# A channel-attention kernel on one core: 398 of 1152 rows kept on chip instead of 392, and the second pass in another order

## The chip, the cores and the metric

The kernel runs on one core of one Trainium2 chip. The metric is the device time of one execution in microseconds (us); a profiled execution also has a trace, whose own span is a little shorter than that execution's time.

## The reference

```python
x: [1, 384, 384, 384] bfloat16      # H x W positions, 384 channels
w1d: [1] bfloat16                   # a one-tap filter over the channels
g = einsum("bhwc->bc", x) / (H * W) # mean of each channel
s = sigmoid(g * w1d[0])
out = x * s[:, None, None, :]
```

Every value of x is needed for s, and every value of x is needed again, times s, for the output.

## The kernel before, in words

x is laid out as 1152 **rows**: one row is 384 channels in each of the 128 partitions, 768 bytes per partition and 98,304 bytes in all. A tile of "128x18432" elements is 48 rows of 384.

**Pass one** loads all 1152 rows. TensorE multiplies each row by a matrix of ones and accumulates the channel sums in one PSUM bank (`sum_rows`, line 292). Rows that stay on chip for pass two are loaded last into their own places, the others pass through ("streamed"). ScalarE then computes s (`s_bf`, line 513).

**Pass two** writes all 1152 rows times s. Rows that were kept are multiplied on VectorE (`scale`, line 527; three pieces on GpSimd) and stored. Streamed rows have to be loaded a second time, into places that stores have set free, multiplied and stored.

**Kept rows** are of two kinds. Raw rows lie as they came. Folded rows lie in groups: three rows w0, w1, w2 take up the bits of a fourth row u, since some exponent bits of the data are nearly always the same. So four rows occupy three, and u's place may be used for something else. `fold` does this in pass one for a **piece** of four u rows (16 rows): VectorE tests (`test`, a TENSOR_SCALAR of line 327, written to Y), makes two fields (line 327, in T) and joins them (line 333), twice; after each test ScalarE sums the tested values into `seen` (line 364), and the next test has to wait for that, since it writes the same place Y. `unfold` takes a piece apart again in pass two. If a test ever failed, GpSimd does the folded rows again at the end (`verdict`, `again`); with this data it does not.

**Places.** `arena` holds the groups, the raw rows and work places T and Y (eight rows each); `annex` is a block of 20 more rows in what is otherwise scratch memory for software DMA. Groups stand in two columns; the bits that one group (BANKED) saves are kept in PSUM, and a last group EXTRA shares the place A.. with it. U, V and W are the u rows of groups 7, 8 and EXTRA, refilled with raw rows after the fold.

**Order.** All DMAs are issued by SP in the order in which the program records them, on one queue. A load waits for the readers of its place, a store for its scaling, and whatever stands behind a waiting DMA waits too. In pass one the order is written out by hand (`BETWEEN`, `group`). In pass two a planner (the `while True` loop) decides it at build time, from modelled costs (`ROW`, `LAT`, ...) and `RULES`: how large a run of free rows must be to be loaded (at most `CAP`), how long the backlog must be, and in how large parts a load is scaled (`PARTS_OF`). The groups are unfolded in the list `order`.

Of the kernel before, what the change touches and what calls it, by code (L numbers as in the profile page):

```python
# [145 lines left out]
def kernel(  # L146
# [11 lines left out]
    nc = tc.nc  # L158
    P = nc.NUM_PARTITIONS
# [11 lines left out]

    PIECE = 4
    PAIR = 2 * PIECE
    PAIRS = 4
# [3 lines left out]
    A = V + PAIR  # L178
    N_A = 39
    T = A + N_A  # L180
# [7 lines left out]
    for i in range(PAIRS):  # L188
# [21 lines left out]
    pieces = [  # L210
        (g, lo, min(m, q - lo))
        for g, (_, q) in enumerate(GROUPS) for m in [q if g == BANKED else PIECE] for lo in range(0, q, m)
    ]

    ones = pool.tile([P, P], bf16, name="ones")
    w_bf = pool.tile([1, 1], bf16, name="w_bf")
    w_sc = pool.tile([P, 1], f32, name="w_sc")
    worst = pool.tile([P, 1], f32, name="worst")
    odd = pool.tile([P, 1], bf16, name="odd")
    arena = pool.tile([P, ROWS, C], bf16, name="arena")  # L220
    annex = nc.alloc_sbuf_tensor_at("annex", [P, N_X, C], bf16, offset=RING).ap()
    s_bf = pool.tile([P, C], bf16, name="s_bf")
    zeros = pool.tile([P, P], bf16, name="zeros")
    seen = pool.tile([P, 2 * len(pieces)], f32, name="seen")
    odd_i = pool.tile([P, 1], mybir.dt.int32, name="odd_i")
# [4 lines left out]
    CUT = C - C // 3  # L230
    tail = bank0[:, nc.PSUM_BANK_SIZE_BYTES // 4 - (C - CUT) // 2 :].bitcast(bf16)
# [5 lines left out]
    assert BANK * len(banks) - PS * C >= CUT  # L237
    spare = banks[-1][:, BANK - CUT :]

    def view(t, r0, n):  # L240
# [5 lines left out]
    def rows(lo, n):  # L246
        return [("a", r) for r in range(lo, lo + n)]
# [88 lines left out]
    def flat(a, p):  # L336
        return arena[:, a : a + p, :].bitcast(u16)
# [4 lines left out]

    def fold(k, T=T, Y=Y):

        g, lo, p = pieces[k]
        first, q = GROUPS[g]
        a, ua = first + 3 * lo, first + 3 * q + lo
        wc = [rows(a + j * p, p) for j in range(3)]
        u, uc = flat(ua, p), rows(ua, p)
        t, tc2 = flat(T, 2 * p), rows(T, 2 * p)  # L350

        def field(i, op, by, mask):
            bits(flat(T + i * p, p), u, op, by, AND, mask, uc, rows(T + i * p, p))

        def test(i, parts):

            at = Y
            for first, n in parts:
                bits(flat(at, n), flat(first, n), AND, 0x7800, XOR, 0x3800, rows(first, n), rows(at, n))
                at += n  # L360
            y = flat(Y, 2 * p)
            fl.add(
                "ACT",
                lambda: nc.scalar.activation(  # L364
                    out=y, in_=y, func=ACTF.Copy, accum_out=seen[:, 2 * k + i : 2 * k + i + 1]
                ),
                reads=rows(Y, 2 * p), writes=rows(Y, 2 * p) + [("seen", 2 * k + i)],
            )

        test(0, [(a, 2 * p)])  # L370
        field(0, SHL, 7, 0x7800)
        field(1, SHL, 11, 0x7800)
        w01 = flat(a, 2 * p)
        join(w01, w01, t, XOR, wc[0] + wc[1] + tc2, wc[0] + wc[1])
        test(1, [(a + 2 * p, p), (ua, p)])
        field(0, SHL, 3, 0x3800)
        field(1, SHR, 1, 0x4000)
        w2 = flat(a + 2 * p, p)
        for i in range(2):
            join(w2, w2, flat(T + i * p, p), XOR, wc[2] + rows(T + i * p, p), wc[2])  # L380


    N_DVE, N_SP = (62, 14), 32

# [67 lines left out]
    PARTS = ((0, CUT, spare, "spare"), (CUT, C, tail, "bank0"))  # L452
    S1, S2, S3 = [(A, 19)], [(A + 19, 19)], [(X, N_X)]

# [8 lines left out]
    def group(g, where):  # L463

        if isinstance(where, list):
            take(g)
            for k in of_group(g):
                fold(k)
            stream_all(where)
        else:  # L470
            k1, k2 = of_group(g)
            take(g, 0, 12)
            take(g, 24, 32)
            fold(k1)
            stream_all(where[0])
            take(g, 12, 24)
            fold(k2)
            stream_all(where[1])

    BETWEEN = [  # L480
        (2, LOW_COLUMN + HIGH), (4, [(A, 38)]),
        (5, [(G0 - 24, 24), (A - 24, 24), *S3]),
        (6, (S1, S2)), (7, ([(A - 24, 24)], S1)),
        (8, (S3, S2)), (EXTRA, []),
    ]
# [18 lines left out]

    for a, n in [(X, N_X), (U, 8), (V, 8), (W + 4, 8), (W + 12, 8), (W + 20, 7), (W, 4), (T, 4), (T + 4, 4), (Y, 4), (Y + 4, 2), (Y + 6, 2)]:
        step = take_raw(a, n)
        if a == Y - 4:
            fl.hold("DVE", 2 * N_DVE[1], step)
# [4 lines left out]
        lambda: nc.scalar.activation(out=s_bf[:], in_=acc, func=ACTF.Sigmoid, scale=w_sc[:, 0:1]),  # L513
        reads=["bank0", "w_sc"], writes=["s_bf"],
    )
# [77 lines left out]
    def verdict():  # L593

        fl.add(
            "DVE",
            lambda: nc.vector.tensor_reduce(out=worst[:], in_=seen[:], op=Op.max, axis=mybir.AxisListType.X),
            reads=[("seen", k) for k in range(2 * len(pieces))], writes=["worst"],
        )
        fl.add(  # L600
            "DVE",
            lambda: nc.vector.tensor_single_scalar(out=odd[:], in_=worst[:], scalar=0.0, op=Op.is_gt),  # L602
            reads=["worst"], writes=["odd"],
        )
        fl.add(
            "PE",
            lambda: nc.tensor.matmul(votes, lhsT=ones[:], rhs=odd[:], start=True, stop=True),  # L607
            reads=["ones", "odd"], writes=["bank0"],
        )
# [8 lines left out]
    def again():  # L618
# [28 lines left out]
    RULES = [  # L647
        (80, 48, 8.0, 24, 9.0, 4.0, 3.5),
        (190, 40, 2.5, 14, 3.0, 5.0, 6.0),
        (430, 64, 6.0, 33, 9.0, 4.0, 2.0),  # L650
        (N_STREAM, 24, 6.0, 33, 16.0, 7.0, 6.0),
    ]
    PARTS_OF = (16, 48)
    BANKS_AT = 2
    N_SPLIT, N_WHOLE = 2, 4
    now = dve_at = 0.0
# [49 lines left out]

    for a, n, end in ((Y, 2, True), (Y + 2, 2, True), (Y + 4, 4, True), (V, 4, True), (V + 4, 4, True), (T, 8, True), (X, 10, True), (X + 10, 10, True), (U, 8, True)):
        landed.append((a, raw(a), n, end))
    landed.append((W, raw(W), 8, True))
    landed.append((W + 8, raw(W + 8), 6, True))  # L710


    alongside = deque()
    t = 1.0
    for a, n in ((A + 26, 4), (A + 30, 4), (A + 34, 5)):
# [70 lines left out]
    while True:  # L786
        MANY, SHORT, FEW, AMPLE, LOW, LAST = next(r[1:] for r in RULES if todo <= r[0])

# [52 lines left out]
        if got and todo < N_STREAM:  # L841
            n, a = max(got)
            left = N_STREAM - todo
            left -= run_of(left - 1)[0]
            n = min(n, CAP, left)
            ahead = backlog()
            behind = storing and sum(m for m, _ in got) < MANY and ahead >= SHORT
            if not behind and (todo or not (landed or alongside or waiting)) and (n >= min(BIG, left) and (n == left or left > CAP) or (ahead < LOW and n >= 8) or ahead < LAST):
                storing = False

                lo = N_STREAM - todo - n
                load(lo, a, n)
                for i in range(a, a + n):
                    idle[i] = False
                parts = [(a + e, lo + e, f - e, f == n) for e, f in split(n, PARTS_OF[not line and not turns])]
                todo += n
                moves.append([now + LAT, n * ROW + PER_LOAD, lambda parts=parts: landed.extend(parts)])
# [45 lines left out]
```

## Time and profile before

| | before |
|---|---|
| median of 3 runs | 713.63 us (713.4 to 714.04) |
| profiled execution: its time, its span | 714.23 us, 712.4 us |
| DMA: bytes, mean rate over the span | 301.34 MB, 423 GB/s |
| read from HBM, written to it | 187.96 MB, 113.25 MB |
| busy: DMA queue of SP / VectorE / TensorE / ScalarE | 99% / 67% / 30% / 17% |

The bytes read are 1152 rows for pass one and 760 for pass two; the bytes written are 1152 rows. The page gives engine shares over the whole span; the two passes have to be told apart by windows of time. "DMA share" is the mean busy share of the 16 DMA engines; it can stand a little above 1.

### The profile page before, as it was taken

Reading aid. Unit: us, or ns where it says so; the run is one execution under the profiler, and the core shown is the slowest. Engines: PE = TensorE matmul, PEld = TensorE weight load, DVE = VectorE, ACT = ScalarE, POOL = GpSimd, SP = SyncE. Lnnn points to the kernel's source line nnn. Section 1 sums busy time; section 2 is a strip of 40 time slices with the busy share of each in tenths; the row PEclk is TensorE's granted clock in tenths of the full one; section 3 lists DMA queues with packets and bytes.
Section 4 is the critical chain, followed back from the end, with each engine's and each line's share of the span. In section 5 each row is a group of like instructions: output and inputs, shape, how many; then the busy total and the mean of one; then the engine's idle time right before and its main releaser. Section 6 shows DMA issues by size and latency. Waiting matters only on the chain.

```text
span 712.4 us, 2053 instructions
## 1 busy us (share of the span) xinstructions
PE 214.5 (30%) x1186; PEld 0.3 (0%) x3; DVE 476.3 (67%) x371; ACT 121.6 (17%) x97; POOL 10.2 (1%) x7
## 2 busy tenths in 40 slices
PE   4686968888887880000000000000000000000000
PEld 0000000000000000000000000000000000000000
DVE  3608250347968947959899989979258914897460
ACT  3706140235746730000000200000000000000000
POOL 0000000000000005000000000000000000000000
PEclk9898989999999995555555555555555555555555
DMA  9999999999999998999999999999999999999997
GB/s 370 443 418 440 429 433 433 433 429 432 426 427 428 434 389 346 393 427 423 430 431 434 428 439 439 430 419 435 445 433 428 437 435 433 430 436 433 425 436 311
DMA packets 17727, 301.34 MB, mean 423 GB/s; under 512 B 1971, under 2 KB 2483, under 8 KB 5811
## 3 DMA queue, kind: packets, MB, share of 16 engines
q1 hardware_dynamic: 17712, 301.21, 99.0%
q8 instruction: 4, 0.07, 0.0%
q14 instruction: 9, 0.07, 0.0%
q10 hardware_dynamic: 2, 0.00, 0.0%
HBM read 187.96 MB, written 113.25 MB: 423 GB/s over the span
## 4 chain that ended last, share of the span: by engine, by line
DMA 71%; DVE 16%; PE 7%; ACT 2%; SPq 0%; issue 0%; DVEq 0%
DMA arena<-in_x_dram 47%; DMA out_dram<-arena 19%; DVE arena L527 10%; PE bank L292 7%; DMA annex<-in_x_dram 3%; DVE arena L327 2%; ACT arena L364 2%; DVE annex L527 2%; DVE arena L333 1%; DMA out_dram<-annex 1%; SPq L286 0%; ACT s_bf L513 0%; SPq L541 0%; SPq L898 0%; DVEq L124 0%
## 5 line engine op out<-in xcount | busy, mean ns | idle before, releaser
L527 DVE TENSOR_TENSOR arena<-arena,s_bf 128x6144 bf16<-128x6144 bf16 (+9 forms) x69 | 212.1, 3114 | 84.4 <-DMA arena<-in_x_dram 73.1
L292 PE MATMUL bank<-arena,ones 128*128 128x384 bf16 x1091 | 197.3, 343 | 39.2 <-DMA arena<-in_x_dram 38.4
L327 DVE TENSOR_SCALAR arena<-arena 128x1536 uint16<-128x1536 uint16 (+4 forms) x198 | 136.9, 745 | 105.5 <-DMA arena<-in_x_dram 97.7
L364 ACT ACTIVATE arena<-arena 128x3072 uint16<-128x3072 uint16 (+1 forms) x38 | 107.6, 2831 | 105.6 <-DVE arena L327 105.5
L607 PE MATMUL bank<-odd,ones 128*128 128x1 bf16 x1 | 0.2, 187 | 385.9 <-DVE odd L602 385.9
L333 DVE TENSOR_TENSOR arena<-arena 128x1536 uint16<-128x1536 uint16 (+3 forms) x83 | 106.6, 1284 | 9.2 <-PE bank L292 6.2
L445 ACT COPY arena<-bank 128x512 uint32<-128x512 uint32 (+3 forms) x9 | 4.5, 497 | 127.1 <-DMA out_dram<-arena 126.9
L527 DVE TENSOR_TENSOR annex<-annex,s_bf 128x3840 bf16<-128x3840 bf16 x6 | 12.7, 2153 | 10.5 <-DMA annex<-in_x_dram 10.5
L527 POOL TENSOR_TENSOR arena<-arena,s_bf 128x1536 bf16<-128x1536 bf16 (+1 forms) x3 | 10.0, 3356 | 268.6 <-ACT bank L517 268.6
L292 PE MATMUL bank<-annex,ones 128*128 128x384 bf16 x60 | 11.9, 361 | 4.5 <-DMA annex<-in_x_dram 4.5
L445 ACT COPY bank<-arena 128x512 uint32<-128x512 uint32 (+3 forms) x9 | 4.1, 491 | 35.8 <-PE bank L292 35.8
L527 DVE TENSOR_TENSOR arena<-arena,bank 128x1536 bf16<-128x1536 bf16 (+2 forms) x7 | 8.2, 1232 | 0.0
L364 ACT ACTIVATION_READ_ACCUMULATOR arena<-arena 128x1 f32 x38 | 7.1, 186 | 0.0
L292 PE MATMUL bank<-zeros,ones 128*128 128x384 bf16 x32 | 5.5, 326 | 0.0
L527 DVE TENSOR_TENSOR annex<-annex,bank 128x3840 bf16<-128x3840 bf16 x2 | 4.2, 2145 | 0.0
L306 PE MATMUL bank<-arena,ones 128*128 128x384 bf16 x1 | 0.5, 479 | 7.8 <-DMA arena<-in_x_dram 7.8
L513 ACT ACTIVATE s_bf<-bank,w_sc 128x384 bf16<-128x384 f32 x1 | 0.6, 581 | 9.7 <-PE bank L292 9.7
L871 ACT ACT_TABLE_LOAD x1 | 1.3, 1283 | 0.7 <-PEq L887 0.7
L396 DVE TENSOR_SCALAR w_sc<-bank 128x1 f32<-128x1 f32 x1 | 0.2, 159 | 1.1 <-PE bank L391 1.1
L386 DVE MEMSET ones<- 128x128 bf16 x1 | 0.2, 165 | 1.0 <-SPq L118 1.0
L391 PE MATMUL bank<-w_bf,ones 1*128 1x1 bf16 x1 | 0.2, 182 | 2.1 <-DMA w_bf<-in_w1d_dram 2.1
L607 PEld LDWEIGHTS bank<-odd,ones 128*128 128x128 bf16 x1 | 0.1, 105 | 643.6 <-DVE odd L602 643.6
(11 smaller groups left out, 1.5 us busy)
## 6 DMA issues: line engine op xcount, KB each, us to landing
arena<-in_x_dram SPq DMA_DIRECT2D x17, 4608.0 KB, 30.2
out_dram<-arena SPq DMA_DIRECT2D x7, 4608.0 KB, 30.0
out_dram<-arena SPq DMA_DIRECT2D x6, 3072.0 KB, 33.0
arena<-in_x_dram SPq DMA_DIRECT2D x5, 3072.0 KB, 15.2
arena<-in_x_dram SPq DMA_DIRECT2D x6, 2304.0 KB, 20.9
annex<-in_x_dram SPq DMA_DIRECT2D x6, 1920.0 KB, 11.0
arena<-in_x_dram SPq DMA_DIRECT2D x2, 4512.0 KB, 25.9
out_dram<-arena SPq DMA_DIRECT2D x2, 4512.0 KB, 18.6
```

The lines of the kernel that those rows point to most:

```text
L292: return pe.add_instruction(mybir.InstMatmult(name=nc.get_next_instruction_name(), ins=[pe.lower_ap(rhs), pe.lower_ap(ones[:])], outs=[pe. ...
L306: return nc.tensor.matmul(acc, lhsT=ones[:], rhs=mem(i, 1)[:, 0, :], start=first, stop=last)
L327: lambda: nc.vector.tensor_scalar(out=dst, in0=src, scalar1=s0, scalar2=s1, op0=op0, op1=op1),
L333: "DVE", lambda: nc.vector.tensor_tensor(out=dst, in0=a, in1=b, op=op), reads=reads, writes=writes
L364: lambda: nc.scalar.activation(out=y, in_=y, func=ACTF.Copy, accum_out=seen[:, 2 * k + i : 2 * k + i + 1]),
L386: fl.add("DVE", lambda: nc.vector.memset(ones[:], 1.0), writes=["ones"])
L391: lambda: nc.tensor.matmul(votes, lhsT=ones[0:1, :], rhs=w_bf[0:1, 0:1], start=True, stop=True),
L445: "ACT", lambda: nc.scalar.copy(dst.bitcast(u32), src.bitcast(u32)), reads=reads, writes=writes
L513: lambda: nc.scalar.activation(out=s_bf[:], in_=acc, func=ACTF.Sigmoid, scale=w_sc[:, 0:1]),
L527: lambda: vec.tensor_tensor(out=v, in0=v, in1=s[:, None, :].to_broadcast([P, n, C]), op=Op.mult),
L607: lambda: nc.tensor.matmul(votes, lhsT=ones[:], rhs=odd[:], start=True, stop=True),
L871: nc.scalar.preload_act_table(ACTF.Sigmoid)
```

## The change

Six more rows are kept, so that 754 instead of 760 rows are loaded twice: EXTRA has eight u rows instead of four (four more rows kept), A is one row longer, and the annex has 21 rows instead of 20, since the DMA scratch (`RING`) shrinks from 1024 to 256 bytes. To make room, small tiles (`ones`, `zeros`, `w_sc`, `seen`, ...) move into parts of `s_bf`, into one small tile and into free PSUM. EXTRA's second fold works in place on one row quarter at a time (`tight`), with Y as its only work place.

In pass one, a group's load is cut otherwise: first the last 20 rows (the second piece's w rows and all u rows), then the first 12; the second piece is folded first. What is streamed between them changes. In pass two the planner has other costs, other rules, with `CAP` and the size of scaled parts now in each rule, and another order of the groups. Core of the diff:

```diff
+    N_EXTRA = 8
-    N_A = 39
+    N_A = 40
-    GROUPS.append((A, PIECE))
-    W = A + 3 * PIECE
+    GROUPS.append((A, N_EXTRA))
+    W = A + 3 * N_EXTRA
+    R = W + N_EXTRA
-    RING, SCRATCH = 1024, 16384
+    RING, SCRATCH = 256, 16384
...
+        if tight:
+            w0, w1, w2 = a, a + p, a + 2 * p
+            parts = ((w2, SHL, 3, 0x3800, w2), (ua, SHR, 1, 0x4000, w2), (w0, SHL, 7, 0x7800, w0), (w1, SHL, 11, 0x7800, w1))
+            for i, (tested, op, by, mask, at) in enumerate(parts):
+                test(2 * k + i if i < 2 else N_SEEN + i - 4, [(tested, p)])
+                field(T, op, by, mask)
+                into(at, p, T)
+            return
...
-    N_DVE, N_SP = (62, 14), 32
+    N_DVE, N_SP = (62, 14), 34
...
-            take(g, 0, 12)
-            take(g, 24, 32)
-            fold(k1)
+            _, lo, _ = pieces[k2]
+            take(g, 3 * lo)
+            fold(k2)
             stream_all(where[0])
-            take(g, 12, 24)
-            fold(k2)
+            take(g, 0, 3 * lo)
+            fold(k1, Y, Y + PIECE, True) if g == EXTRA else fold(k1)
             stream_all(where[1])
...
-    LAT, SEEN, DT = 2.0, 1.5, 0.05
-    PENDING, MERGE = 24.0, 8.0
-    BIG, CAP = 32, 48
+    LAT, SEEN, DT = 1.5, 1.5, 0.05
+    PENDING, MERGE = 24.0, 16.0
+    BIG = 40
     RULES = [
-        (80, 48, 8.0, 24, 9.0, 4.0, 3.5),
...
+        (65, 90, 6.0, 24, 12.0, 3.0, 3.5, 40, 40),
...
+        (N_STREAM, 110, 8.0, 49, 4.0, 4.0, 4.0, 96, 32),
     ]
-    PARTS_OF = (16, 48)
-    N_SPLIT, N_WHOLE = 2, 4
+    N_SPLIT, N_WHOLE = 1, 2
...
-    (c0, c1), N_NEAR = COLUMNS, 2
-    order = [c0[-1], c0[-2], c0[-3], EXTRA, BANKED, c1[-1], c0[-4], c1[-2], c1[-3], c1[-4], FIRST]
+    (c0, c1), N_NEAR = COLUMNS, 3
+    order = [c0[-1], c0[-2], c1[-1], c1[-2], EXTRA, c0[-3], c1[-3], BANKED, c0[-4], FIRST, c1[-4]]
```

Counted over the whole program, SP issues 123 transfers before and 126 in the changed kernel, a load of 96 rows (128x2x18432) counted twice since it is one transfer in two pieces per partition; 51 of them are in pass one in both.

**Place one: the last loads of pass one, on SP.** `f_PE`, `f_DVE` and `f_ACT` are waits for TensorE, VectorE and ScalarE. Before, the rows from 128x2688 on go to W, T and Y:

```order
L286 DMA arena<-in_x_dram 128x6144 [waits f_PE]
L286 DMA annex<-in_x_dram 128x7680 [waits f_PE]
L286 DMA arena<-in_x_dram 128x3072 [waits f_DVE] x2
L286 DMA arena<-in_x_dram 128x3072 [waits f_PE] x2
L286 DMA arena<-in_x_dram 128x2688 [waits f_PE]
L286 DMA arena<-in_x_dram 128x1536 [waits f_PE,f_DVE]
L286 DMA arena<-in_x_dram 128x1536 [waits f_DVE] x2
L286 DMA arena<-in_x_dram 128x1536 [waits f_ACT]
L286 DMA arena<-in_x_dram 128x768 x2
```

In the changed kernel the last 128x4608 is EXTRA's first 12 rows, and the loads from the last [waits f_DVE] pair on go to W and Y:

```order
L288 DMA arena<-in_x_dram 128x4608 [waits f_PE]
L288 DMA arena<-in_x_dram 128x3072 [waits f_PE] x2
L288 DMA arena<-in_x_dram 128x3072 [waits f_DVE]
L288 DMA annex<-in_x_dram 128x4224 [waits f_PE]
L288 DMA annex<-in_x_dram 128x3840 [waits f_PE]
L288 DMA arena<-in_x_dram 128x6144 [waits f_DVE,f_PE]
L288 DMA arena<-in_x_dram 128x3072 [waits f_PE] x2
L288 DMA arena<-in_x_dram 128x1536 [waits f_DVE]
L288 DMA arena<-in_x_dram 128x1536
L288 DMA arena<-in_x_dram 128x1536 [waits f_DVE]
L288 DMA arena<-in_x_dram 128x768 [waits f_ACT]
L288 DMA arena<-in_x_dram 128x768
```

After EXTRA's last load, 93 rows are still to come now and 79 before. The load that waits for the last step of the last fold (a join on VectorE) has 12 rows from its start to the end of the pass before and 8 now; the load that waits for the step before that one has 16 in both.

**Place two: the first second loads of pass two, on SP.** `f_SPn` is a wait for an earlier DMA to have landed. Before, from the last three of the stores that come first:

```order
L541 DMA out_dram<-arena 128x1920 [waits f_POOL]
L541 DMA out_dram<-arena 128x3072 [waits f_DVE]
L541 DMA out_dram<-arena 128x2304 [waits f_DVE]
L286 DMA annex<-in_x_dram 128x7680 [waits f_SP10,f_SP12]
L286 DMA arena<-in_x_dram 128x10368 [waits f_SP11,f_SP14,f_SP8,f_SP15,f_SP16]
L541 DMA out_dram<-arena 128x4608 [waits f_DVE]
L541 DMA out_dram<-annex 128x3840 [waits f_DVE] x2
```

In the changed kernel, from the last two of them:

```order
L547 DMA out_dram<-arena 128x1920 [waits f_POOL]
L547 DMA out_dram<-arena 128x1152 [waits f_DVE]
L288 DMA annex<-in_x_dram 128x4224 [waits f_SP11]
L288 DMA annex<-in_x_dram 128x3840 [waits f_SP12]
L288 DMA arena<-in_x_dram 128x6144 [waits f_SP10,f_SP8,f_SP14,f_SP15]
L547 DMA out_dram<-arena 128x4608 [waits f_DVE]
L547 DMA out_dram<-annex 128x4224 [waits f_DVE]
L547 DMA out_dram<-annex 128x3840 [waits f_DVE]
L547 DMA out_dram<-arena 128x6144 [waits f_DVE]
```

The store of 12 rows (128x4608) is the first piece that VectorE has unfolded. Ahead of it stand 79 rows of stores and 47 of loads before, 69 and 37 now.

**Place three: the last DMAs, on SP.** Before:

```order
L286 DMA arena<-in_x_dram 128x18048 [waits f_SP18]
L286 DMA arena<-in_x_dram 128x16512 [waits f_SP19]
L541 DMA out_dram<-arena 128x12288 [waits f_DVE]
L541 DMA out_dram<-arena 128x6144 [waits f_DVE]
L541 DMA out_dram<-arena 128x18048 [waits f_DVE]
L541 DMA out_dram<-arena 128x16512 [waits f_DVE]
```

In the changed kernel:

```order
L547 DMA out_dram<-arena 128x24192 [waits f_DVE]
L547 DMA out_dram<-arena 128x18816 [waits f_DVE]
L288 DMA arena<-in_x_dram 128x2x18432 [waits f_SP17,f_SP18]
L288 DMA arena<-in_x_dram 128x29184 [waits f_SP19,f_SP21]
L288 DMA arena<-in_x_dram 128x16512 [waits f_SP0,f_SP20]
L547 DMA out_dram<-arena 128x2x18432 [waits f_DVE]
L547 DMA out_dram<-arena 128x29184 [waits f_DVE]
L547 DMA out_dram<-arena 128x16512 [waits f_DVE]
```

The last loads are of 96, 76 and 43 rows instead of 47 and 43, and all unfolded rows are stored ahead of them. Over pass two the queue turns from loads to stores or back 22 times before and 20 times now.

More of the change, by code (lines that the diff above doesn't have):

```diff
@@ L210 @@
     pieces = [
-        (g, lo, min(m, q - lo))
-        for g, (_, q) in enumerate(GROUPS) for m in [q if g == BANKED else PIECE] for lo in range(0, q, m)
-    ]
[L215 to L219, printed above, removed]
+        (g, max(0, lo), min(q, lo + m) - max(0, lo))
+        for g, (_, q) in enumerate(GROUPS) for m in [q if g == BANKED else PIECE] for lo in range(-(-q % m), q, m)
+    ]
+    s_bf = pool.tile([P, C], bf16, name="s_bf")
+    ones, zeros = s_bf[:, 0:P], s_bf[:, P : 2 * P]
+    small = pool.tile([P, 8], f32, name="small")
+    w_sc, worst, cell, last = (small[:, i : i + 1] for i in range(4))
+    w_bf, odd = cell.bitcast(bf16)[0:1, 0:1], cell.bitcast(bf16)[:, 1:2]
+    odd_i = last.bitcast(mybir.dt.int32)
     arena = pool.tile([P, ROWS, C], bf16, name="arena")
     annex = nc.alloc_sbuf_tensor_at("annex", [P, N_X, C], bf16, offset=RING).ap()
[L222 to L225, printed above, removed]
     bank0 = psum.tile([P, nc.PSUM_BANK_SIZE_BYTES // 4], f32, name="bank0")
@@ L229 @@
     BANK = nc.PSUM_BANK_SIZE_BYTES // 2
-    CUT = C - C // 3
+    N_SEEN = 2 * len(pieces) + 2
+    CUT = 2 * C // 3 - 2 * N_SEEN
     tail = bank0[:, nc.PSUM_BANK_SIZE_BYTES // 4 - (C - CUT) // 2 :].bitcast(bf16)
@@ L238 @@
     spare = banks[-1][:, BANK - CUT :]
+    free = BANK * len(banks) - PS * C - CUT
+    seen = banks[-1][:, BANK - CUT - free : BANK - CUT].bitcast(f32)[:, 0:N_SEEN]
     def view(t, r0, n):
@@ L341, with fold @@
     )
-    def fold(k, T=T, Y=Y):
+    def fold(k, T=T, Y=Y, tight=False):
         g, lo, p = pieces[k]
@@ L347, in fold, with field @@
         a, ua = first + 3 * lo, first + 3 * q + lo
-        wc = [rows(a + j * p, p) for j in range(3)]
         u, uc = flat(ua, p), rows(ua, p)
-        t, tc2 = flat(T, 2 * p), rows(T, 2 * p)
-        def field(i, op, by, mask):
-            bits(flat(T + i * p, p), u, op, by, AND, mask, uc, rows(T + i * p, p))
+        def field(at, op, by, mask):
+            bits(flat(at, p), u, op, by, AND, mask, uc, rows(at, p))
         def test(i, parts):
@@ L513 @@
         lambda: nc.scalar.activation(out=s_bf[:], in_=acc, func=ACTF.Sigmoid, scale=w_sc[:, 0:1]),
[L514 removed]
+        reads=["bank0", "w_sc"], writes=["s_bf", "ones", "zeros"],
     )
@@ L597, in verdict @@
             lambda: nc.vector.tensor_reduce(out=worst[:], in_=seen[:], op=Op.max, axis=mybir.AxisListType.X),
-            reads=[("seen", k) for k in range(2 * len(pieces))], writes=["worst"],
+            reads=[("seen", k) for k in range(N_SEEN)], writes=["worst"],
         )
@@ L604, in verdict @@
         )
+        again_ones = arena[:, T, 0:P]
+        fl.add("DVE", lambda: nc.vector.memset(again_ones, 1.0), writes=rows(T, 1))
         fl.add(
             "PE",
-            lambda: nc.tensor.matmul(votes, lhsT=ones[:], rhs=odd[:], start=True, stop=True),
-            reads=["ones", "odd"], writes=["bank0"],
+            lambda: nc.tensor.matmul(votes, lhsT=again_ones, rhs=odd[:], start=True, stop=True),
+            reads=rows(T, 1) + ["odd"], writes=["bank0"],
         )
@@ L704, in stored @@
         return f
[L707 removed]
+    for a, n, end in ((Y, 2, True), (Y + 2, 2, True), (Y + 4, 4, True), (V, 4, True), (V + 4, 4, True), (T, 8, True), (X, 11, True), (X + 11, N_X - 11, True), (U, 8, True)):
         landed.append((a, raw(a), n, end))
[L709 to L710 removed]
+    landed.append((W, raw(W), A + 27 - W, True))
     alongside = deque()
     t = 1.0
[L715 removed]
+    for a, n in ((A + 27, 4), (A + 31, 4), (A + 35, 5)):
         scale(a, n, "POOL", after=[copied])
@@ L854 @@
                     idle[i] = False
-                parts = [(a + e, lo + e, f - e, f == n) for e, f in split(n, PARTS_OF[not line and not turns])]
+                parts = [(a + e, lo + e, f - e, f == n) for e, f in split(n, PART)]
                 todo += n
```

46 lines of the change are left out of this document (20 added, 26 removed), and 2 rows, old and new, of the table RULES.

## Prediction

> **What bounds the kernel now.** I read the page first: the span, the DMA rows of the 40 slices, the queue, the bytes, and the chain that ended last.
>
> ```profile
> span 712.4 us, 2053 instructions
> ...
> DMA  9999999999999998999999999999999999999997
> GB/s 370 443 418 440 429 433 433 433 429 432 426 427 428 434 389 346 393 427 423 430 431 434 428 439 439 430 419 435 445 433 428 437 435 433 430 436 433 425 436 311
> ...
> q1 hardware_dynamic: 17712, 301.21, 99.0%
> ...
> HBM read 187.96 MB, written 113.25 MB: 423 GB/s over the span
> ...
> DMA 71%; DVE 16%; PE 7%; ACT 2%; SPq 0%; issue 0%; DVEq 0%
> ```
>
> The one queue that SP feeds takes 99% of the time of all 16 DMA engines. Only the first slice, the turn between the passes (slices 15 to 17) and the last slice are lower. The kernel is a stream of bytes with two short holes and two ends. Windows of time give their sizes; the last two columns are DMA share and GB/s.
>
> ```profile
> 4.00:258.00 254.00, 204.70 (x1132) 0.10 (x1) 144.00 (x190) 114.61 (x84) 0.00 (x0) 0.93 1.00 431
> 120.00:160.00 40.00, 35.91 (x218) 0.00 (x0) 14.81 (x20) 11.64 (x9) 0.00 (x0) 1.00 1.00 433
> 220.00:260.00 40.00, 33.40 (x181) 0.00 (x0) 34.11 (x47) 26.43 (x20) 0.00 (x0) 0.91 1.01 427
> 265.00:270.00 5.00, 2.71 (x15) 0.00 (x0) 1.39 (x3) 0.90 (x2) 0.99 (x1) 1.00 0.22 84
> 270.00:272.00 2.00, 0.00 (x0) 0.00 (x0) 2.00 (x3) 0.00 (x0) 2.00 (x1) 0.53 0.86 330
> 290.00:340.00 50.00, 0.00 (x0) 0.00 (x0) 41.19 (x31) 0.00 (x0) 0.00 (x0) 0.50 1.01 418
> 290.00:685.00 395.00, 0.19 (x1) 0.10 (x1) 309.44 (x160) 4.48 (x9) 0.00 (x0) 0.50 1.00 430
> 500.00:685.00 185.00, 0.19 (x1) 0.10 (x1) 119.62 (x51) 0.00 (x0) 0.00 (x0) 0.50 1.00 433
> 707.00:712.40 5.40, 0.00 (x0) 0.00 (x0) 0.00 (x0) 0.00 (x0) 0.00 (x0) 0.50 0.06 26
> ```
>
> From 4 to 258 and from 290 to 685 us the engines are full (share 1.00) at 431 and 430 GB/s. The turn leaves them idle for 78% of 5 us, 3.9 us; after 707 almost nothing moves. At 430 GB/s a row of 98,304 bytes takes 0.2286 us. The check: pass two moves 1912 rows (760 in, 1152 out), 437.1 us; its data starts at 270, so it ends at 707.1, where the last window begins. No other loss is left in it. Yet SP waits all the time:
>
> ```profile
> SPq L541 <- DVE arena L527: 251.0, 33, 25.4
> SPq L286 <- DMA out_dram<-arena: 98.6, 14, 10.9
> ```
>
> SP stands for 251 us behind VectorE before stores and 98.6 us before loads, while the engines work off what it issued earlier. So the question about every wait is how many rows are queued behind it. A wait costs nothing until that is used up, and from there each microsecond costs one.
>
> **What the change takes away and adds in bytes and transfers.** Pass one still loads 1152 rows in 51 transfers, so it is worth nothing in bytes. Pass two moves 6 rows less: 6 x 0.2286 = 1.37 us. It issues 75 transfers instead of 72. What does a transfer cost beside its bytes? In pass one, 120 to 160 us has transfers of 42 rows on average and 433 GB/s (0.2270 us a row), 220 to 260 us has 13 rows and 427 GB/s (0.2302): 0.0032 / (1/13 - 1/42) = 0.06 us a transfer. In pass two, 500 to 685 us has 45 rows and 433 GB/s, 290 to 340 us has 17 rows and 418 GB/s (0.2352): 0.0082 / (1/17 - 1/45) = 0.22 us, which also holds the turns of the queue between loads and stores. Three transfers are 0.18 to 0.67 us. I take 0.25, near the lower row, since the turns fall from 22 to 20.
>
> [...]
>
> Larger pieces: no transfer before is over 48 rows (36,864 bytes per partition), and now some 840 rows go in transfers of 49 to 96. No row shows their rate. The nearest are 433 and 430 GB/s: I take no difference, and 1% either way of 840 x 0.2286 us, 1.9 us, as bounds.
>
> **What it moves, at the three places where the queue could run dry.** *The end of pass one.* One more piece is folded. The rows of the chain of folds: its first test after a wait for data, its last step, the test's sum on ScalarE at two sizes, and a step of four rows on VectorE; then, from the chain of waits, SP's issue of the loads that waited for the end.
>
> ```profile
> 198.92 0.96 DVE L327 TENSOR_SCALAR arena<-arena 128x3072 uint16<-128x3072 uint16 x1 [3.09 <-DMA arena<-in_x_dram]
> ...
> 258.12 0.19 ACT L364 ACTIVATION_READ_ACCUMULATOR arena<-arena 128x1 f32 x1
> ```
>
> ```profile
> L364 ACT ACTIVATE arena<-arena 128x3072 uint16<-128x3072 uint16 x36 | 99.5, 2763 | 93.6 <-DVE arena L327 93.5
> L327 DVE TENSOR_SCALAR arena<-arena 128x1536 uint16<-128x1536 uint16 x132 | 66.0, 553 | 7.4 <-ACT arena L364 2.8 <-DMA out_dram<-arena 2.3 <-DMA arena<-in_x_dram 0.8
> L364 ACT ACTIVATE arena<-arena 128x4608 uint16<-128x4608 uint16 x2 | 8.1, 4044 | 11.9 <-DVE arena L327 11.9
> ```
>
> ```profile
> 258.24 0.33 SPq L286
> ```
>
> Seven pieces, groups 6, 7, 8 and EXTRA, take 258.31 - 198.92 = 59.4 us, 8.5 each, waits for TensorE included. Now there are eight, but group 6 starts after 817 loaded rows instead of 861: 44 x 0.2286 = 10.1 us earlier, at 188.8. Seven at 8.5 end at 248.3. The eighth goes in four quarters: 0.55 on VectorE, then on ScalarE an estimated 1.48 (4044 - 2763 = 1281 ns for four more rows, and a start of 0.2) and 0.19; four times 2.2 is 8.9, so the fold ends at 257.2, 1.1 us earlier. Data of pass one ends at about 266.1 (265 plus 22% of 5). The first load that waits has 16 rows, 3.7 us, from there, and needs about 1 us from issue to data: it may be issued at 261.4. Reserve 4 us; this costs nothing. If a piece took 9 us it would be gone. The turn itself keeps its chain: last row, sigmoid, first scaling, first store.
>
> *The first unfolded piece in pass two.* VectorE waits until the rows of U have been stored, then unfolds:
>
> ```profile
> 284.93 1.50 DVE L327 TENSOR_SCALAR arena<-arena 128x1536 uint16<-128x1536 uint16 x3 [2.32 <-DMA out_dram<-arena]
> 286.46 1.95 DVE L333 TENSOR_TENSOR arena<-arena 128x1536 uint16<-128x1536 uint16 x2
> 288.33 1.35 DVE L327 TENSOR_SCALAR arena<-arena 128x4608 uint16<-128x4608 uint16 x1
> 289.71 2.56 DVE L527 TENSOR_TENSOR arena<-arena,s_bf 128x4608 bf16<-128x4608 bf16 x1
> 292.30 0.34 SPq L541 DMA_DIRECT2D out_dram<-arena  x1
> ```
>
> That store is issued at 292.30, and its data can flow at about 293.3. Ahead of it 126 rows are queued, at 0.2352 us a row until 299.6: reserve 6.3 us. Now U's rows are one row later in the queue, so the data can flow at 293.6, and only 106 rows stand ahead, until 294.9. **Reserve 1.3 us**: nothing is lost, but this is the tightest place. Next is the store of the 16 rows of the third load: landed by about 295, scaled in 3.35 us, at 299.5 in the queue, which lasts until 302.7.
>
> *The end.* The store of 96 rows waits for two scalings of 48.
>
> ```profile
> L527 DVE TENSOR_TENSOR arena<-arena,s_bf 128x6144 bf16<-128x6144 bf16 x26 | 85.9, 3353 | 53.1 <-DMA arena<-in_x_dram 53.1
> L527 DVE TENSOR_TENSOR arena<-arena,s_bf 128x12288 bf16<-128x12288 bf16 x5 | 32.8, 6559 | 0.2
> ```
>
> 16 rows take 3.35 and 32 take 6.56 us, so 48 take an estimated 9.77 and both 19.5 us. Behind the load of 96 rows the loads of 76 and 43 are queued, 119 rows or 27.2 us. Reserve 7.7 us, less about 4 for the landing and the issue. Then 76 rows take 15.5 us on VectorE against 21.9 us that the store of 96 lasts. Nothing is lost here.
>
> **The sum.** -1.37 + 0.25 = -1.1 us. The profiled execution of 714.23 us (span 712.4) would take 713.1. It lies 0.6 us above the median of 713.63; against that median the forecast is **712.5 us**.
>
> **The rivals.** About 0.2% of the time, 1.4 us, is what a measurement of this kernel can tell from no change; so faster means below 712.2 and slower above 715.1.
>
> *A, the likeliest, 0.63: the stream stays full.* 712.5, from 711.2 to 713.6: 0.4 for the transfers, about 1 for the larger pieces.
>
> *B, 0.19: the tail or the early stage gets shorter too.* After the stream's end one burst is left:
>
> ```profile
> 707.00:708.00 1.00, 0.00 (x0) 0.00 (x0) 0.00 (x0) 0.00 (x0) 0.00 (x0) 0.50 0.16 66
> ...
> 709.00:710.00 1.00, 0.00 (x0) 0.00 (x0) 0.00 (x0) 0.00 (x0) 0.00 (x0) 0.50 0.15 66
> ```
>
> A few packets still move at 709 to 710, so some engine is 2 to 3 us behind the others. If another order evens that out, up to 2 us go; if 290 to 340 us ran at 433 instead of 418 GB/s, 50 x 15/433 = 1.7 us. With one of them: 710.8. For it speaks that two turns of the queue fall away; against it, that the first loads become smaller (11 and 10 rows for 20).
>
> *C, 0.15: the queue runs dry at the first unfolded piece, slower than before.* Its reserve falls from 6.3 to 1.3 us. If that store came 5 us later than worked out, the loss would be 3.7 and the time 712.5 + 3.7 = 716.2; it beats the bytes saved from 2.4 us of lateness on, and shows as slower from 3.9 us on. For it: VectorE is the engine that SP waits for (251 us), and 41.19 of 50 us busy from 290 to 340, so a delay is not soon made up. Against it: the steps before are the same, with measured durations.
>
> [...]
>
> **Chances.** Faster: B, and 0.35 of A: 0.19 + 0.22 = 0.41. Slower: D and most of C (0.11): 0.14. Same: the rest, 0.45, with the mild part of C. The range leaves out C's and D's larger half and the end of B: 710.9 to 714.6.
>
> **What would show it.** Right: bytes read 187.37 MB; share 1.00 at about 430 GB/s in all of pass two; a turn of 3.9 us at the same place; a last slice as now. Wrong: a share below 0.95 in a window near 295 us (C), between 258 and 265 us (the folds came late), or near 650 us (the 96 rows came late); other GB/s in the stage of the larger transfers; a shorter or longer tail after the last store's stream (B).

## The result, and the profile after

| | before | changed |
|---|---|---|
| median (5 runs each) | 713.63 us | 716.93 us (716.5 to 717.89) |
| ratio | | 1.0046, 95% interval 1.0033 to 1.0059 |
| profiled execution: time, span | 714.23, 712.4 us | 717.89, 716.1 us |

The change makes the kernel slower by about 3.3 us; the forecast was 712.5 us, a gain of 1.1, in a range of 710.9 to 714.6. The profiled execution is the slowest of the five, 1 us above their median. Its page, in the rows that were shown of before:

```profile
span 716.1 us, 2033 instructions
...
DMA  9999999999999997999999999999999999999996
GB/s 371 436 417 439 427 432 434 428 430 426 424 431 423 424 386 304 391 430 419 428 425 430 434 426 434 446 417 456 412 441 427 438 413 444 432 435 423 429 439 295
...
q1 hardware_dynamic: 18112, 300.62, 98.6%
...
HBM read 187.37 MB, written 113.25 MB: 420 GB/s over the span
```

The bytes are as forecast, and the stream is still low only at its two ends and at the turn. The windows of time (last columns: TensorE's clock, DMA share, GB/s) say where it lost:

```profile
4.00:258.00 254.00, 200.36 (x1123) 0.11 (x1) 152.14 (x202) 119.57 (x92) 0.00 (x0) 0.94 1.00 429
...
265.00:270.00 5.00, 5.00 (x32) 0.00 (x0) 0.00 (x0) 0.00 (x0) 0.00 (x0) 1.00 0.49 184
270.00:272.00 2.00, 0.87 (x6) 0.00 (x0) 0.39 (x1) 0.90 (x2) 0.08 (x1) 1.00 0.00 0
290.00:340.00 50.00, 0.00 (x0) 0.00 (x0) 47.31 (x30) 0.00 (x0) 0.00 (x0) 0.50 1.01 417
290.00:685.00 395.00, 0.19 (x1) 0.10 (x1) 319.03 (x128) 4.47 (x9) 0.00 (x0) 0.50 1.01 430
```

Pass two is full at 430 GB/s, as before. Pass one is full too, but at 429 GB/s where it had 431, and it still moves data in 49% of the window from 265 to 270 us, where it had 22%. The turn's own chain, in the timeline (start, duration, engine), first of before, then of the changed kernel:

```profile
267.99 0.58 ACT L513 ACTIVATE s_bf<-bank,w_sc 128x384 bf16<-128x384 f32 x1 [9.69 <-PE bank L292]
...
268.61 0.56 DVE L527 TENSOR_TENSOR arena<-arena,s_bf 128x768 bf16<-128x768 bf16 x1 [10.39 <-ACT s_bf L513]
```

```profile
270.90 0.58 ACT L519 ACTIVATE s_bf<-bank,small 128x384 bf16<-128x384 f32 x1 [12.72 <-PE bank L294]
...
271.61 0.56 DVE L533 TENSOR_TENSOR arena<-arena,s_bf 128x768 bf16<-128x768 bf16 x1 [13.53 <-ACT s_bf L519]
```

The sigmoid starts 2.91 us later; from it to the first scaling 0.71 us pass instead of 0.62. So pass one itself ends later. Each transfer leaves 16 landing records, read here as one for each of the 16 DMA engines, and what waits for it goes on after the last of them: the first matmul on pass one's last rows starts at 267.47 us in before and 270.38 in the changed kernel, 0.04 us after the slowest landing. These records give this table for all kernels of this study, from one profiled execution of each. "Past 256" is how far the arena's base address in SBUF lies past a multiple of 256 bytes; "mean" and "last" are the landing of pass one's last load, as a mean over the 16 engines and on the slowest; "first store" is the landing of pass two's first store on the median engine, "last store" that of its last on the slowest.

```
kernel                       base   past 256   mean    last    first store  last store
before                      16896      0      266.37  267.43    270.94      710.67
e8_before_fetch_early       16896      0      267.08  268.40    271.92      711.53
e2_new_plan_392             16896      0      266.87  267.45    270.95      721.05
e11_before_256              16640      0      266.55  267.67    271.19      710.58
e9_aligned_256              16640      0      266.32  267.53    272.68      711.37
e13_kept_warm               16640      0      266.70  267.59    271.11      709.35
e14_warm_fetch_late_loads   16640      0      266.32  268.34    271.91      710.60
changed kernel              17312    160      267.85  270.34    273.97      714.73
e1_old_plan                 17312    160      267.69  269.99    273.61      713.75
e3_dve_padding_48           17312    160      267.67  269.20    276.07      715.53
e4_pitch_717                17312    160      267.78  270.53    274.16      712.87
e5_arena_aligned            17344    192      267.80  270.54    274.15      715.09
e7_aligned_and_fetch        17344    192      267.73  269.06    272.61      711.17
e6_before_shifted           16928     32      269.44  270.10    273.66      715.90
e10_before_off_32           16672     32      268.87  269.78    273.31      714.73
e12_396_shifted             16672     32      268.10  269.53    274.50      715.78
```

The last load lands 2.91 us later: 1.48 on the mean engine, and 1.43 because the slowest is further behind it (2.49 us against 1.06). Then follow 0.12 in the turn, -0.43 for pass two on the median engine, +1.46 because the slowest engine is further behind the median at the end too, and -0.40 in the tail: 3.7 us of span, less rounding.

### The profile page after: what moved, and what is told of

It reads as the page before. It is cut to its first block, busy times and chain, and to the rows that moved or that the text cites. A ratio compares the mean times of both kernels' runs of the same rounds, so it can differ in the third digit from the quotient of the medians.

```text
span 716.1 us, 2033 instructions
## 1 busy us (share of the span) xinstructions
PE 212.9 (30%) x1186; PEld 0.3 (0%) x3; DVE 485.1 (68%) x346; ACT 126.4 (18%) x105; POOL 10.2 (1%) x7
## 4 chain that ended last, share of the span: by engine, by line
DMA 42%; DVE 34%; PE 11%; another core or an unknown queue 7%; issue 1%; SPq 0%; DVEq 0%
DMA arena<-in_x_dram 31%; DVE arena L533 22%; PE bank L294 11%; DMA out_dram<-arena 10%; DVE arena L329 6%; DVE arena L335 4%; DVE annex L533 2%; SPq L547 0%; SPq L288 0%; DVEq L126 0%; PE bank L615 0%; DVE small L619 0%; DVE small L608 0%; DVE arena L612 0%
## 5 line engine op out<-in xcount | busy, mean ns | idle before, releaser
L533 DVE TENSOR_TENSOR arena<-arena,s_bf 128x9216 bf16<-128x9216 bf16 (+14 forms) x37 | 205.0, 5567 | 75.4 <-DMA arena<-in_x_dram 61.2
L329 DVE TENSOR_SCALAR arena<-arena 128x1536 uint16<-128x1536 uint16 (+5 forms) x201 | 142.9, 767 | 110.9 <-DMA arena<-in_x_dram 90.5
L294 PE MATMUL bank<-arena,s_bf 128*128 128x384 bf16 x1067 | 191.5, 342 | 44.6 <-DMA arena<-in_x_dram 44.0
L364 ACT ACTIVATE arena<-arena 128x3072 uint16<-128x3072 uint16 (+2 forms) x42 | 113.5, 2702 | 110.0 <-DVE arena L329 110.0
L335 DVE TENSOR_TENSOR arena<-arena 128x1536 uint16<-128x1536 uint16 (+3 forms) x85 | 111.7, 1314 | 8.5 <-PE bank L294 5.2
L533 DVE TENSOR_TENSOR annex<-annex,s_bf 128x4224 bf16<-128x4224 bf16 (+2 forms) x7 | 17.6, 2553 | 0.2 <-DMA annex<-in_x_dram 0.2
L294 PE MATMUL bank<-annex,s_bf 128*128 128x384 bf16 x84 | 16.0, 350 | 4.1 <-DMA annex<-in_x_dram 4.1
L533 DVE TENSOR_TENSOR arena<-arena,bank 128x1536 bf16<-128x1536 bf16 (+3 forms) x7 | 7.2, 1092 | 0.0
L294 PE MATMUL bank<-s_bf 128*128 128x384 bf16 x32 | 5.5, 326 | 0.0
L533 DVE TENSOR_TENSOR annex<-annex,bank 128x4224 bf16<-128x4224 bf16 (+1 forms) x2 | 4.4, 2250 | 0.0
L308 PE MATMUL bank<-arena,s_bf 128*128 128x384 bf16 x1 | 0.5, 479 | 7.3 <-DMA arena<-in_x_dram 7.3
```

Of the source, the lines that this page charges most:

```text
L294: return pe.add_instruction(mybir.InstMatmult(name=nc.get_next_instruction_name(), ins=[pe.lower_ap(rhs), pe.lower_ap(ones[:])], outs=[pe. ...
L308: return nc.tensor.matmul(acc, lhsT=ones[:], rhs=mem(i, 1)[:, 0, :], start=first, stop=last)
L329: lambda: nc.vector.tensor_scalar(out=dst, in0=src, scalar1=s0, scalar2=s1, op0=op0, op1=op1),
L335: "DVE", lambda: nc.vector.tensor_tensor(out=dst, in0=a, in1=b, op=op), reads=reads, writes=writes
L364: lambda: nc.scalar.activation(out=y, in_=y, func=ACTF.Copy, accum_out=seen[:, i : i + 1]),
L533: lambda: vec.tensor_tensor(out=v, in0=v, in1=s[:, None, :].to_broadcast([P, n, C]), op=Op.mult),
```

## The experiments

Times are medians; each batch of four (two in the last) has its own runs of before. In a diff, "..." stands for lines left out.

**Is it the order of pass two?** e1 is the changed kernel with the planner of before (its costs, rules and order); e2 is the reverse, before with the new planner.

```diff
-    order = [c0[-1], c0[-2], c1[-1], c1[-2], EXTRA, c0[-3], c1[-3], BANKED, c0[-4], FIRST, c1[-4]]
+    order = [c0[-1], c0[-2], c0[-3], EXTRA, BANKED, c1[-1], c0[-4], c1[-2], c1[-3], c1[-4], FIRST]
...
```

> The changed kernel (398 rows, its pass one) with the second pass planned by the old costs, rules and order of groups. Theory L (the time is lost in pass one, before the turn, and by the slowest of the 16 DMA engines): the turn stays 3 us late (first store about 274 instead of 270.9), so the time stays near the changed kernel, 715.5 to 717.5. Rival P (the new order of pass two costs it): the time falls to about 713.

> The kernel before (392 rows, its pass one) with the new planner costs, rules and order of groups in pass two. Theory L: pass one and the turn are as before, so the time is 713 to 714.6, no more than 1 us from before. Rival P: about 716.5, as the changed kernel.

Before gave 714.30 here. e1: 716.98 us, ratio 1.0036 (1.0025 to 1.0048): the loss stays when the new order goes. e2: 724.25, 1.0129 (1.0111 to 1.0146), which neither theory expected. Its windows show the queue empty near its end, since a last load has no other work behind it that would cover its landing (704.8 us) and the first of its two scalings (to 709.2):

```profile
700.00:705.00 5.00, 0.00 (x0) 0.00 (x0) 0.14 (x1) 0.00 (x0) 0.00 (x0) 0.50 0.41 178
705.00:710.00 5.00, 0.00 (x0) 0.00 (x0) 5.00 (x2) 0.00 (x0) 0.00 (x0) 0.50 0.00 0
```

The new plan does not suit 392 rows; of 398 e2 tells nothing, except that its pass one ends as in before.

**Which part of pass one?** The changed kernel with 14 fewer padding waits on VectorE (e3; waits that only move the place of what follows in VectorE's program), and with the run of streamed rows cut so that a partition's rows lie 717 rows apart as before, not 711 (e4).

```diff
-    N_DVE, N_SP = (62, 14), 34
+    N_DVE, N_SP = (48, 14), 34
```

```diff
-    N_FIRST = 43
+    N_FIRST = 37
```

> The changed kernel with 48 instead of 62 padding waits at the start of VectorE's program, so that the first scaling of pass two has the same place in VectorE's instruction stream as before, and the fetch of its next block of instructions (seen at 254.65 us, inside the last loads; at 268.79 in the turn's hole before) moves into the turn. Theory L: the last load of pass one lands about 1 us earlier, 715.9. Rival: fetches are hidden and nothing moves, 716.9.

> The changed kernel with the first run of rows cut at 37 instead of 43, so that the main streamed run has 717 rows per partition as before, not 711. Rival H (the rows' stride in HBM makes the loads of pass one 0.4% slower, 10.93 instead of 10.89 us per 48 rows): the middle DMA engine ends pass one 1.2 us earlier, 715.7. Theory L without it: no change, 716.9.

e4: 717.21, 1.0034 (1.0024 to 1.0045); the mean engine ends at 267.78, so the pitch does nothing. e3: 719.62, 1.0071 (1.0054 to 1.0087), slower still. Its last load lands 1.1 us earlier than the changed kernel's, but the turn then lost 3.2 us:

```profile
270.77 6.45 POOL L533 TENSOR_TENSOR arena<-arena,s_bf 128x1536 bf16<-128x1536 bf16 x2 [270.33 <-ACT bank L523]
270.81 3.46 DVE L533 TENSOR_TENSOR arena<-arena,s_bf 128x768 bf16<-128x768 bf16 x1 [12.91 <-ACT bank L523]
```

GpSimd's scaling started 0.04 us ahead of VectorE's, and VectorE's took 3.46 us in place of 0.56. In seven other kernels (before, changed, e7, e9, e12, e13, e14) VectorE started 0.31 to 0.41 us first, and its scaling took 0.56. In e3 a second run of padding waits, released by the load to Y, ended only at 270.77 us, 0.43 us after the sigmoid, so VectorE came late. What e3 moved is seen in the records of the instruction fetches. These have DMA queues of their own on the page: q14 with blocks of 8192 bytes, q8 with 16384. A block on q14 moves with VectorE's padding and is taken for VectorE's. It comes at 268.8 us in before, in the empty turn. In the changed kernel it came at 254.7, among the last loads, and the slowest engine's lag behind the median jumps there from 1.90 to 2.88 us within one transfer; in e3 it came at 271.2 and there is no jump. The same holds for all kernels of the table, those of the later experiments too:

```
kernel                       fetch    slowest behind median, transfer before and at the fetch
changed kernel               254.65   1.90  2.88
e1_old_plan                  254.30   1.56  2.54
e4_pitch_717                 254.84   2.04  3.03
e5_arena_aligned             254.80   2.02  2.99
e8_before_fetch_early        257.61   0.79  1.59
e14_warm_fetch_late_loads    253.82   1.44  2.44
the ten others         268.5 to 272.3   rises by 0.06 at most in the last eleven loads
```

So the author takes it that one of the engines that move the data moves the fetch too; the records do not name the engine. The fetch's record lasts 0.31 us in before and 0.32 in the changed kernel; why an engine falls back by 0.8 to 1.0 is open.

**The address of the arena.** To make room, the change also moved small tiles, and with them the arena's base. e5 moves the base of the changed kernel by 32 bytes, e6 that of before. e7 is e5 with the fetch moved into the turn and the second run of padding waits released one load earlier, so that VectorE's first scaling is ahead of GpSimd's again; e8 moves the fetch of before among the last loads.

```diff
-    small = pool.tile([P, 8], f32, name="small")
+    small = pool.tile([P, 16], f32, name="small")     # e5, e7
-    N_DVE, N_SP = (62, 14), 34
+    N_DVE, N_SP = (48, 14), 34                        # e7
-        if a == Y:
+        if a == W + 4:                                # e7
```

```diff
+    pad = pool.tile([P, 8], f32, name="pad")          # e6, ahead of the arena
-    N_DVE, N_SP = (62, 14), 32
+    N_DVE, N_SP = (76, 14), 32                        # e8
```

> The changed kernel, with 32 unused bytes ahead of the arena, so that its base lies at 17344 (a multiple of 64) in place of 17312 (32 above one); before it lay at 16896 (a multiple of 512). Every load and store goes to or from the arena or the annex. Theory D (the start address of a row in SBUF sets a small part of the cost of every row): the median DMA engine ends pass one near 266.3, as before, in place of 267.5, and pass two too gets back up to 0.7 us; the slowest engine still lags by 2.8 us because the fetch of VectorE's instructions still falls among the last loads; time 715.0 to 715.7. Rival N (the order and sizes of the loads, or the folds beside them, make the drift): median end 267.5 and time 716.9, unchanged.

> The kernel before with 32 unused bytes ahead of the arena: its base goes from 16896 to 16928, 32 above a multiple of 64, as in the changed kernel. Nothing else is moved. Theory D: the median DMA engine ends pass one near 267.4 in place of 266.3, and the time is 714.9 to 715.6. Rival N: 713.6 to 714.3, as before.

> The kernel of e5_arena_aligned with VectorE's first padding 48 waits in place of 62 and the second padding released by the load W + 4, three loads before the end of pass one, where before it stood. Theory F (the fetch of VectorE's next instructions takes the DMA engine that then ends pass one last): the fetch moves from 255 us into the turn, the slowest engine's lag at the end of pass one falls from 2.8 to 1.9 us, GpSimd's first scaling starts behind VectorE's, and the time is 1.0 below that of e5: with theory D 714.0 to 714.7, without it 715.7 to 716.0. Rival C (the lag is chance, the fetch costs nothing): the same time as e5.

> The kernel before with VectorE's first padding 76 waits in place of 62: the fetch of its next instructions moves from the turn (268.8 us) to about 256 us, among the last loads of pass one, and nothing else is moved there. Theory F: the slowest engine's lag at the end of pass one rises from 1.15 to some 2.1 us and the time by up to 1.0, to 714.3 to 715.3. Rival C: 713.6 to 714.3, the lag near 1.2.

Before gave 714.93 here. e5: 717.04, 1.0029 (1.0016 to 1.0042), its pass one unchanged: a multiple of 64 does not help, the expectation was wrong. e6: 718.41, 1.0049 (1.0030 to 1.0067): 32 unused bytes cost before as much as the whole change did. e7: 715.79, 1.0010 (0.9998 to 1.0022), 1.25 below e5, with last load and first store 1.5 us earlier (0.97 of it is the jump that e5 has and e7 has not). e8: 715.18, 1.0005 (0.9994 to 1.0017): the lag jumps from 0.79 to 1.59 at the fetch, but the time can't be told from before's nor from the forecast.

**Is 256 bytes the measure?** e9 is e7 on a multiple of 256; that costs two kept rows, since the arena then leaves no room for `s_bf`, which moves below the annex, and the annex gives up two. e12 is e9 shifted by 32. e11 is before on a multiple of 256 that is none of 512 (`ones` goes behind the arena); e10 is e11 shifted by 32.

```diff
-    s_bf = pool.tile([P, C], bf16, name="s_bf")
+    s_bf = nc.alloc_sbuf_tensor_at("s_bf", [P, C], bf16, offset=RING).ap()   # e9, e12
-    X, N_X = ROWS + 1, (SCRATCH - RING) // (2 * C)
+    X, N_X = ROWS + 1, 19                                                    # e9, e12
-    small = pool.tile([P, 16], f32, name="small")
+    small = pool.tile([P, 32], f32, name="small")                            # e9; e12: 40
...
```

> The kernel of e7_aligned_and_fetch with the arena's base at 16640, a multiple of 256 (before: 16896, one too; the changed kernel 17312 and e7 17344, none). To make room, the scale tile goes to address 256 and the annex keeps 19 rows in place of 21, so that 396 rows are kept. Theory D in its second form (a row whose SBUF address is no multiple of 256 costs more to transfer): the mean DMA engine ends pass one at 266.4 to 267.0 in place of 267.7, and with 2 rows more to read (0.46) the time is 0.9 to 1.6 below e7: 714.2 to 714.9 where before gives 714.9 and e7 gives 715.8. Rival N (orders and sizes of the loads): 267.7 and 716.2.

> The kernel of e9_aligned_256 with the arena 32 bytes further, at 16672; nothing else is changed. Theory D: slower than e9 by 1.4 to 3.4 us (the price of 160 bytes past a multiple of 256 in the changed kernel at the end of pass one, and of 32 bytes in e6 over the whole run), most of it by the end of pass one. Rival N: the same time as e9 within 0.5 us.

> The kernel before with the tile of ones behind the arena in place of ahead of it and 32 unused bytes ahead: the arena's base at 16672, again 32 past a multiple of 256, at another place in memory than in e6 (16928). Theory D: slower than before by 2 to 3.5 us as e6 was, mean engine at the end of pass one near 268.5 to 269.5. Rival (e6 was slow for another reason): as before, 714.9.

> The kernel before with the tile of ones behind the arena: base 16640, a multiple of 256 but not of 512. Theory D with 256 bytes as the measure: no change, 714.5 to 715.3 beside 714.9, mean engine at the end of pass one 266.3 to 267.1. Rival (the measure is 512 bytes, or any shift of the arena costs): slower by 1 to 3 us.

Before gave 714.37. e9: 714.26, 0.9997 (0.9985 to 1.0010). e12: 717.57, 1.0043 (1.0028 to 1.0057). e10: 718.58, 1.0057 (1.0042 to 1.0071). e11: 714.44, 1.0006 (0.9997 to 1.0015). In both geometries 32 bytes cost 3.3 to 4.1 us. A multiple of 256 is enough (e11), one of 64 is not (e5); no base on a multiple of 128 that is none of 256 was run, so 128 is not excluded as the measure. The rate over the loads from 20 to 250 us shows the price directly; first e11, then e10:

```profile
20.00:250.00 230.00, 189.58 (x1052) 0.00 (x0) 127.54 (x172) 102.34 (x78) 0.00 (x0) 0.92 1.00 431
```

```profile
20.00:250.00 230.00, 185.16 (x1046) 0.00 (x0) 125.30 (x168) 100.20 (x77) 0.00 (x0) 0.93 1.00 427
```

Both at share 1.00, at 431 and 427 GB/s: the engines are as busy and move less. Over 230 us that is 2.1 us. In e9 the last load lands as in before, yet its first store is 1.7 us later. Its timeline of TensorE and a window:

```profile
254.55 3.33 PE L294 MATMUL bank<-annex,s_bf 128*128 128x384 bf16 x19 [1.07 <-DMA annex<-in_x_dram]
260.06 9.64 PE L294 MATMUL bank<-arena,s_bf 128*128 128x384 bf16 x48 [2.18 <-DMA arena<-in_x_dram]
```

```profile
260.00:265.00 5.00, 4.94 (x21) 0.66 1.01 413
```

After 2.18 us without work TensorE ran at 0.66 of its clock, so the sums of the last 48 rows ended 2.2 us behind the last load. The forecast of e9 had no such loss in it; that its time was met even so is luck. That 160 or 192 bytes past have their price from the address, too, rests on e7 against e9, where `s_bf`, the annex and two rows changed with it; for 32 bytes the address alone was changed.

**Taking that away, and the fetch once more.** e13 is e9 with ten matmuls on zeros in the gap; e14 is e13 with the fetch back among the last loads.

```diff
+        if a == R:
+            keep_warm(10)                              # e13, e14
...
-    N_DVE, N_SP = (48, 14), 34
+    N_DVE, N_SP = (62, 14), 34                         # e14
```

> The kernel of e9_aligned_256 with ten matmuls on zeros ahead of the sums of the 16 rows at R, so that TensorE has some 0.6 us without work there in place of 2.18. Theory W (after 2.18 us without work the clock fell to 0.66, so the sums of the last 48 rows took 9.64 us and ended 2.2 us behind the last load): the sums end within 0.6 us of the last load, the first store comes at 271.0 in place of 272.7, and the time is 1.6 below e9: 712.4 to 713.0 where before gives 714.4, which is the gain of the four kept rows and a little more. Rival (the sums are late for another reason): 714.3, as e9.

> The kernel of e13_kept_warm with VectorE's first padding 62 waits in place of 48, so that the fetch of its next instructions falls among the last loads again (near 255 us) and not into the turn. Theory F (the fetch takes one DMA engine from the loads): the slowest engine's lag at the end of pass one is up to 1.0 us larger and the time 0.5 to 1.0 above e13: 712.9 to 714.0. Rival C (the lag is chance): the same as e13 within 0.3 us.

Before gave 714.94. e13: **712.31**, 0.9965 (0.9953 to 0.9977), faster than both kernels. e14: 714.07, 0.9988 (0.9976 to 1.0000). Both came out within 0.1 us of the forecast ranges, but those assumed 714.4 for before: beside its own before, e13 gained 0.6 us more than forecast. TensorE in e13:

```profile
257.77 1.79 PE L294 MATMUL bank<-s_bf 128*128 128x384 bf16 x10
260.12 7.99 PE L294 MATMUL bank<-arena,s_bf 128*128 128x384 bf16 x48 [0.56 <-DMA arena<-in_x_dram]
```

The 48 sums take 7.99 us in place of 9.64. In e14 the lag jumps from 1.44 to 2.44 us at the fetch (253.8 us), the last load lands 0.75 later than in e13 and the first store 0.80; the medians lie 1.76 apart, so the fetch accounts for about half and the rest is not shown.

## Why the prediction was wrong

*The step that failed* is "Pass one still loads 1152 rows in 51 transfers, so it is worth nothing in bytes", taken as nothing in time. Bytes and transfers were the same, the price of a transfer was not. The small tiles that the diff moves to make room moved the arena from a multiple of 256 to 160 past one. The mean engine's end separates the kernels without overlap: 266.3 to 267.1 us in the seven on a multiple of 256, 267.7 to 269.4 in the nine others. Of the changed kernel's loss, 1.48 us stands here. The lag of the slowest engine adds 1.43: one fetch is 0.9 to 1.0 of it, and the rest, which stood before that fetch, is not explained.

The runs fit 256 bytes as the measure (e11 at 714.44 us against e10 at 718.58; e5, on a multiple of 64, at 717.04); what makes such a start dearer they do not show. Nor does the price grow with the offset: 32 bytes cost 1.8 to 3.1 us of pass one (e12 against e9, e10 against e11, e6 against before), 160 or 192 about 1.4 (the changed kernel against before, e7 against e9).

*"The turn itself keeps its chain"* held (3.63 us from last landing to first store, 3.51 before), but when it starts is set by the slowest of 16 engines, and a fetch had been moved out of the turn among the last loads, where that engine fell back by 0.98 us at one transfer. VectorE has 336 instructions ahead of its first scaling where it had 322, and without 14 of them (e3) the fetch comes at 271.2 us in place of 254.65; no row that the prediction read shows that. In the turn the fetch leaves no mark on the lag (e7, e13: it rises by 0.06 us at most); among the last loads of a full queue it does (e14: 1.44 to 2.44).

*Rows:* 1.37 less 0.25 was forecast for pass two. On the median engine it takes 437.27 us before; five kernels with 398 rows and the new plan take 436.84 (changed), 436.14 (e3), 436.51 (e4), 436.05 (e5) and 436.25 (e7), 0.4 to 1.2 less, 0.9 on average. Within that scatter this term was right.

*Rival C* (queue dry at the first unfolded piece) did not happen, although its 716.2 us lies near the measured 716.93; that is chance. Its store went out at 295.86 us, 3.6 later than before, of which 3.0 are the turn's, and the queue stayed full:

```profile
291.00:297.00 6.00, 0.00 (x0) 0.00 (x0) 5.96 (x4) 0.00 (x0) 0.00 (x0) 0.50 1.01 426
```

The folds ended at 258.2 us (forecast 257.2). The 96 rows were scaled in 19.45 us (forecast 19.5), and near 650 us the share is 0.99. Of the terms in the reserves, the 1 us from issue to data was 0.92 in before (first store: 269.19 to 270.11); the 4 us for landing and issue at the end was the author's estimate, and the 96 rows took 3.83 from the median engine's landing to the slowest (635.03 to 638.86), beside 0.9 from issue to data. *D*, a constant that every transfer pays, stands in the chances with 0.03: no run shows such a constant, and pass two, with 75 transfers in place of 72, ran full at 430 GB/s as before. *Rival B* looked at the right place, an engine behind the others at the end, and had the sign wrong: there it grew from 2.47 to 3.93 us. That last 1.46 us is not explained; over the runs of this study the lag at the end lies between 0.7 and 4.9 us.

So with the address, the fetch and the clock put right (e13, four rows more than before), the gain is there: 2.5 us where four rows, at 0.2286 for each load saved, give 0.9. The remainder lies in a shorter tail and a smaller lag and was not taken apart.

## What to carry to other kernels

In this kernel, whose DMA queue stayed full, "the same bytes" was not "the same time": look where the buffers start (32 bytes past a multiple of 256 cost 3.3 to 4.1 us here), and whether an unrelated edit of the layout moves them. The end of pass one belonged to the slowest of the 16 engines (2.49 us behind the mean in the changed kernel), so look what falls among the last loads, and try an instruction fetch in a hole that exists anyway (e13 is 1.76 us below e14, the lag's jump about half of it). A loss of this kind is found by undoing one byte offset or one padding at a time, since the engines' busy share read 1.00 either way (e10, e11).

## What the hardware did that was not expected

- A start 32 bytes past a multiple of 256 costs more than one 160 or 192 past it: 1.8 to 3.1 us (e6, e10, e12) against 1.4 us (e7, the changed kernel) on 51 loads. Why is open.
- A fetch of 8192 bytes of VectorE's instructions (q14) among full loads went with one engine falling back by 0.8 to 1.0 us at that transfer (six kernels of six).
- An operation on VectorE that started 0.04 us behind one on GpSimd took 3.46 us in place of 0.56 (e3, one profiled execution).
- TensorE's clock fell within the stretch after 2.18 and 2.24 us without work (e9, e12; 0.66 and 0.76 of full speed in the window from 260 to 265 us), and did not after 1.92, 2.02 and 2.05 us (e7, e5, e14). In the changed kernel it did after 2.01 us (0.81 from 255 to 260), where the late loads hid it. So the length of the gap alone does not decide it.
